# Where the weight combinations of a Strassen-like product are made, which engine starts the v loads, and the order of the five products

## The chip, the cores and the metric

The kernel runs on one core of a Trainium2 chip. The metric is device time in microseconds of one launch. The kernel before took 1371.44 us, the median of 3 runs (1368.53 to 1373.01).

## What is computed

Three layers follow one another, all in float32. B = 8, H = 8, S = 576, D = 64; 4608 tokens of width 512.

```
attention in chunks of 64 positions, per head:
  scores = q_c @ k_c^T / 8;  attn = softmax(scores);  a = attn @ v_c
x  = a as [4608, 512]
h  = x @ moe_w_in            # 512 -> 2048
g  = max(h, 0) + log1p(exp(-|h|))        # softplus
x2 = g @ moe_w_out           # 2048 -> 512
h2 = max(x2 @ w1, x2 @ w2, x2 @ w3)      # 512 -> 768, three times
out = h2 @ moe2_w_out        # 768 -> 512
```

The weights of the layers come in as 64-bit floats.

## The kernel before

A float32 number is kept as two float32r parts, hi and lo; a product is three matmul passes, hi x hi, hi x lo and lo x hi. The tokens are cut into 9 blocks of 512. TensorE's work is written in this order:

1. Blocks 0 to 2 run the first feed-forward layer plainly (mlp1), beside attention and beside the conversion of the weights from 64 bits.
2. Blocks 3 to 8 are three pairs, q = 0, 1, 2 (strassen, line 1690). The first matrix product of a pair (x @ w_in) is done in 8 units of 7 half-size products each (UnitA), with combined weights that lie in DRAM (wac, wae) and are loaded for each pair by GpSimd's queue into a ring. Between the units stand, for pairs 0 and 1, the output products of the pair's first block (mlp1_out), and after the units those of the second block; for that second block the activations go to DRAM and come back (gd). In some units a group of attention products is put in (attention(..., apart=True)).
3. For pair 2 the second matrix product (g @ w_out) is done by seven products too (class Sevens, line 1246): two of them (along) beside the units, the other five (step) after them, each in four parts n2 = 0 to 3. They are named 5, 6, 3, 4 and 7 and run in that order. Each needs activation differences, made on VectorE from raw tiles (split), and weights of its own: for 5, 6, 7 and 3 these are sums and differences of quarters of w_out, made by combos (line 1192) and stored to DRAM as wso; for 4 they are a plain quarter of w_out, which combos stores to DRAM as well. step loads them on SyncE (line 1314) into a ring of 6.
4. The gated layer takes three blocks at a time (class Triple) in 15 products, with weights combined by weights3 on VectorE and ScalarE: once for the first third of the columns (after the mark FIRST, the fifth unit of pair 1), once for the rest (after product 5 begins). They are stored as w2c; GpSimd's queue loads them again (line 1541). After the 15 products come the output products (line 1656), and the result is written.

SBUF holds 46 equal slots of 512 KB, with smaller pools beside them; a tile gets a slot of an allowed kind ("w" 32, "x" 8, "z" 4, "qh" and "vh" one each) and gives it back after its last use.

The order on each engine is not the order of the source. Each step is entered in a plan (class Plan, line 58) with a cost per engine, a latency, transfers with their time on a queue, and a due time. order() then runs a simulated clock: whenever an engine is free, the ready step with the earliest due time starts. A step without a due time gets one from those that need it. `after=` orders steps on this clock alone; at run time only the data are waited for. TensorE's steps are chained in one line. Queues run in the order given to them: what stands behind a waiting transfer on SyncE or GpSimd waits too.

For the groups of attention products, q and k are loaded in a transposing pattern of 128-byte runs on SyncE, v in 256-byte runs on GpSimd (line 468, from the call in line 687); there is one v buffer, which comes free when the product of the tile before is done. The softmax result goes through DRAM and back on SyncE (pd).

The four groups of weight combinations are put in after the output products 1, 4, 7 and 10 of pair 0:

```
    COMBOS = (1, 4, 7, 10)
    MORE = (3, 0), (5, 0), (5, 0)
    FIRST = ("unit", 1, 4)
...
                if q == 0 and j in COMBOS:
                    combos(COMBOS.index(j), [o], clock[0] + 15.0)
```

Of the kernel before, what the change touches and what calls it, by code (L numbers as in the profile page):

```python
# [20 lines left out]
P = 128  # L21
# [162 lines left out]
def tile_kernel(ctx: ExitStack, tc: tile.TileContext, q, k, v, w_in, w_out, w1, w2, w3, wo2, out):  # L184
# [110 lines left out]
    NP = 3  # L295
# [238 lines left out]

    def softmax(sc, pbuf, by_head=False):
        mx, sm = Buf("mx"), Buf("mx")
# [3 lines left out]
        if sc is None:  # L540
            s3 = lambda e: XZ.t[e][:, :TB // 2].rearrange("p (c k) -> p c k", k=CH)
            for h in range(2):
                op(
                    {"D": 0.42},
                    lambda e, h=h: nc.vector.reduce_max(m4()[:, h], s3(h), axis=AX.X),
                    r=[(XZ, "XZ"[h])],
                    w=[(mx, h)],
                    alloc=[] if h else [mx, sm],
                )
            for h in range(2):  # L550
                tt_op(
                    lambda h=h: p4()[:, h],
                    lambda h=h: s3(h),
                    lambda h=h: m4()[:, h, :, None].to_broadcast([P, HP, CH]),
                    ALU.subtract,
                    [(XZ, "XZ"[h]), (mx, h)],
                    [(pbuf, h)],
                    n=0.6,
                    alloc=[] if h else [pbuf],
                )  # L560
        else:
            s4 = lambda: sc.t[:, :, :TB // 2].rearrange("p e (c k) -> p e c k", k=CH)
            op({"D": 0.69}, lambda e: nc.vector.reduce_max(m4(), s4(), axis=AX.X), r=[(sc, "s")], w=[mx], alloc=[mx, sm])
            if by_head:
                op({"D": 0.1}, lambda e: nc.vector.tensor_scalar(mx.t, mx.t, -SCALE, -DROP, ALU.mult, ALU.add), w=[mx])

                def heads(e):
                    for u in range(H):
                        nc.scalar.activation(
                            p3()[:, u], s4()[:, u // HP, u % HP], AF.Softplus, bias=mx.t[:, u:u + 1], scale=SCALE  # L570
                        )

                op({"A": 1.9}, heads, r=[(sc, "s"), mx], w=[pbuf], alloc=[pbuf])
            else:
                tt_op(
                    p4, s4, lambda: m4()[:, :, :, None].to_broadcast([P, 2, HP, CH]), ALU.subtract, [(sc, "s"), mx], [pbuf], alloc=[pbuf]
                )
        if not by_head:
            op({"A": 0.62}, lambda e: nc.scalar.activation(pbuf.t, pbuf.t, AF.Softplus, bias=drop[:, :1], scale=SCALE), w=[pbuf])
        op({"D": 0.69}, lambda e: nc.vector.reduce_sum(sm.t, p3(), axis=AX.X), r=[pbuf], w=[sm])  # L580
        op({"D": 0.1}, lambda e: nc.vector.tensor_scalar(sm.t, sm.t, 1e-9 * float(np.exp(-DROP)), None, ALU.add), w=[sm])
# [94 lines left out]
    def attention(t, after=(), apart=False):  # L676

        if t < NTILE:
# [192 lines left out]
    def weights3(late, after):  # L871
# [31 lines left out]
        def put(s, r):  # L903
# [72 lines left out]
    SEVENS = (2,)  # L976
    COMBOS = (1, 4, 7, 10)
    MORE = (3, 0), (5, 0), (5, 0)
# [208 lines left out]
    def raw_of(q, n, f, h):  # L1187
        if (q, n // 2, f, h) not in raws:
            raws[q, n // 2, f, h] = slot("x", "w", "z", dt=F32)
        return raws[q, n // 2, f, h]  # L1190

    def combos(n2, after, due):
# [4 lines left out]
        for f in range(2):  # L1197
            for nn in range(2):
# [11 lines left out]
                if f == nn == 0:  # L1210
                    in_line("pairo", o)
                if f:
                    store["s", 4, n2, nn] = op(
                        {"G": 1.0},
                        lambda e, w=w, nn=nn: nc.gpsimd.dma_start(out=wso[4][n2][:, :, nn, :], in_=w.t[:, :, HT:].bitcast(F32)),
                        r=[w],
                        after=after,
                        lat=2.0,
                        move=1.1,
                    )  # L1220
        two_of = lambda f, h: (lambda: R[f].t[:, :, h * HT:(h + 1) * HT])
        tv = lambda: t.t.rearrange("p (n c) -> p n c", n=2)

        def put(p, src, r):
            z = slot("w", "x", "z")
            hi, lo = (lambda l=l: z.t[:, l].rearrange("p (n c) -> p n c", n=2) for l in range(2))
            copy_op(hi, src, r, [(z, "h")], alloc=[z])
            tt_op(lo, src, lambda: hi().bitcast(F32), ALU.subtract, r + [(z, "h")], [(z, "l")], hold=[token], due=due)
            store["s", p, n2] = op(
# [16 lines left out]
    class Sevens:  # L1246
# [36 lines left out]
        def send(u, name, b, h):  # L1283
# [3 lines left out]
            )  # L1287

        def split(u, p, n2):
            R = {(f, h): raws[u.q, n2, f, h] for f in range(2) for h in range(2)}  # L1290
            at, src = {
                5: ((0, 0), ((0, 1), (0, 0))),
                6: ((0, 0), ((1, 1), (0, 0))),
                3: ((1, 1), ()),
                4: ((1, 0), ((1, 0), (0, 0))),
                7: ((0, 1), ((1, 1), (0, 1))),
            }[p]
            z = R[at]
            if src:
                a, b = (R[k] for k in src)  # L1300
                tt_op(lambda: wide(z.t), lambda: wide(a.t), lambda: wide(b.t), ALU.subtract, [a, b], [z], n=1.77)
            GH, GL, token = *(Buf("g", "x", "w", fresh=tile_or_slot) for _ in range(2)), Buf("ts")
            o = copy_op(lambda: wide(GH.t), lambda: wide(z.t), [z], [GH], n=1.65, alloc=[token, GH, GL])
            in_line("ts", o)
# [3 lines left out]
        def step(u, p, n2):  # L1308
            GH, GL, token = u.split(p, n2)
            at = {5: 0, 6: 1, 7: 2, 3: 3, 4: 4}[p]  # L1310
            z, ring = slot("w", "x"), Buf("ringo")
            o = op(
                {"S": 0.48},
                lambda e: nc.sync.dma_start(out=z.t.bitcast(F32), in_=wso[at][n2].rearrange("p w n c -> p w (n c)")),
                w=[z],
                alloc=[ring, z],
                after=([store["s", at, n2]] if at < 4 else [store["s", 4, n2, nn] for nn in range(2)]) + [mark["sevens", u.q]],
                lat=2.0,
                move=2.2,
            )  # L1320
            in_line("ringo", o)
            bufs = {5: u.y, 3: u.y, 6: u.acc[:1], 7: u.acc[:1], 4: u.acc[1:]}[p]
# [3 lines left out]
            def fn(e):  # L1326
                for m in range(2):
                    for nn in range(2):
                        for wi, gi in PASS:
                            nc.tensor.matmul(  # L1330
                                dst(m),
                                z.t[:, wi, nn * HT + m * P:nn * HT + (m + 1) * P],
                                (GH, GL)[gi].t[:, nn],
# [4 lines left out]

            o = mark["step", p, n2] = pe2(2.72, fn, r=[z, GH, GL], w=bufs, alloc=[b for b in bufs if b.first is None], hold=[ring, token])
            if n2 == NJ // 4 - 1:  # L1340
# [3 lines left out]
        def read(u, p, bufs):  # L1344
# [10 lines left out]
            if p == 5:  # L1355
                keep(22)
            elif p == 6:
                keep(12)
# [120 lines left out]
    class Triple:  # L1479
# [47 lines left out]
        def product(u, s, d, alloc=()):  # L1527
# [162 lines left out]
    def strassen():  # L1690
# [19 lines left out]
        for q in range(pairs):  # L1710
# [123 lines left out]
    for n, (b, j, first, last) in enumerate(steps):  # L1834
        if n >= NJ and n % (NJ // HP) == 0:
            t = HP + n // (NJ // HP)
            t = 2 * HP + (n - NJ) // 2
            while tiles <= t + 1 and tiles < 22:
                attention(tiles, [first_loads[tiles if tiles < 2 * HP + 3 else NJ - 1]])
                tiles += 1  # L1840
        h = mlp1(b, j, first, last)
        if b == NP - 1 and j % 2 == 0:
            weightsa(j // 2, [before_last], lead)
# [41 lines left out]
```

## Time and profile before

| | |
|---|---|
| median of 3 runs | 1371.44 us (1368.53 to 1373.01) |
| the profiled execution, its own time | 1368.65 us |
| its span in the trace | 1366.8 us |
| TensorE busy | 1331.3 us, 97% |
| VectorE, ScalarE, GpSimd busy | 1002.6, 505.8, 323.9 us |
| moved by DMA | 293.56 MB, 215 GB/s over the span |

The profile is one execution. A span begins with the first instruction and ends with the last; the execution's own time is 1.85 us more. Line numbers are those of the kernel; most copies and sums are made by two helpers, lines 281, 283 (copies) and 288 (sums, differences), so that a row is told by its tiles: s is a slot, g and tmp small tiles, acc, ph, one and both accumulators. "issue" is time in which an engine waited for nothing that the profile shows.

### The profile page before, as it was taken

Reading aid. Unit: us, or ns where it says so; the run is one execution under the profiler, and the core shown is the slowest. Engines: PE = TensorE matmul, PEld = TensorE weight load, DVE = VectorE, ACT = ScalarE, POOL = GpSimd, SP = SyncE. Lnnn points to the kernel's source line nnn. Section 1 sums busy time; section 2 is a strip of 40 time slices with the busy share of each in tenths; the row PEclk is TensorE's granted clock in tenths of the full one; section 3 lists DMA queues with packets and bytes.
Section 4 is the critical chain, followed back from the end, with each engine's and each line's share of the span. In section 5 each row is a group of like instructions: output and inputs, shape, how many; then the busy total and the mean of one; then the engine's idle time right before and its main releaser. Section 6 shows DMA issues by size and latency. Waiting matters only on the chain.

```text
span 1366.8 us, 22719 instructions
## 1 busy us (share of the span) xinstructions
PE 1331.3 (97%) x8616; PEld 1091.1 (80%) x8616; DVE 1002.6 (73%) x1551; ACT 505.8 (37%) x793; POOL 323.9 (24%) x568
## 2 busy tenths in 40 slices
PE   5899999999999999999999999999999999999998
PEld 3788888888888778777788887888888888888886
DVE  8999976797676998658958897879714597145951
ACT  4544333354433544335535553432123222132211
POOL 2011545542233324323231122121101122011100
PEclk9899999999999999999999999999999999999999
DMA  8655567676788999887886799655644465344301
GB/s 273 172 165 156 126 194 202 192 261 212 202 246 258 286 327 294 266 282 257 337 296 223 249 345 364 232 192 208 212 149 162 139 231 202 143 147 154 139 30 63
DMA packets 220253, 293.56 MB, mean 215 GB/s; under 512 B 121984, under 2 KB 147008, under 8 KB 220144
## 3 DMA queue, kind: packets, MB, share of 16 engines
q0 software_dynamic: 54400, 180.31, 38.3%
q1 hardware_dynamic: 164928, 111.02, 27.0%
q8 instruction: 68, 1.11, 0.3%
q10 hardware_dynamic: 816, 0.79, 0.2%
q14 instruction: 41, 0.34, 0.1%
HBM read 198.71 MB, written 93.32 MB: 214 GB/s over the span
## 4 chain that ended last, share of the span: by engine, by line
PE 86%; DMA 6%; DVE 5%; SPq 2%; issue 1%; ACT 0%; POOL 0%; DVEq 0%; ACTq 0%; POOLq 0%
PE acc L1558 14%; PE both L1558 13%; PE acc L816 9%; PE acc L1410 9%; PE ph L796 9%; PE ph L1109 8%; PE one L1109 6%; PE both L1656 6%; PE acc L1656 5%; PE acc L1330 2%; PE acc L1263 2%; DVE s L288 2%; DMA rk<-in_k_dram 1%; PE ph L1330 1%; PE aps L503 1%
## 5 line engine op out<-in xcount | busy, mean ns | idle before, releaser
L288 DVE TENSOR_TENSOR s<-s,s 128x1024 fp32r<-128x1024 f32 (+3 forms) x216 | 208.7, 990 | 24.9 <-ACT s L281 11.7
L1410 PE MATMUL acc<-g,s 128*128 128x512 f32 x768 | 184.8, 393 | 3.7 <-DVE g L288 3.7
L1410 PEld LDWEIGHTS acc<-g,s 128*128 128x128 f32 x768 | 142.6, 188 | 35.8 <-DVE g L288 5.8
L1109 PE MATMUL ph<-s,s 128*128 128x512 f32 x576 | 144.3, 390 | 3.0 <-DMA s<-wac 2.1
L796 PE MATMUL ph<-s,s 128*128 128x512 f32 x576 | 141.2, 396 | 0.0
L816 PE MATMUL acc<-g,s 128*128 128x512 f32 x576 | 139.6, 391 | 0.0
L1109 PEld LDWEIGHTS ph<-s,s 128*128 128x128 f32 x576 | 107.9, 188 | 26.2 <-DMA s<-wac 2.6
L796 PEld LDWEIGHTS ph<-s,s 128*128 128x128 f32 x576 | 108.8, 190 | 23.4
L816 PEld LDWEIGHTS acc<-g,s 128*128 128x128 f32 x576 | 107.4, 188 | 22.7
L1541 POOL DMA_DIRECT2D s<-w2c x105 | 55.9, 532 | 278.1 <-PE both L1558 87.5
L281 ACT CAST g<-s 128x1024 fp32r<-128x1024 f32 (+1 forms) x68 | 62.2, 914 | 159.8 <-PE both L1558 36.3
L1558 PE MATMUL acc<-s,s 128*128 128x512 f32 x452 | 120.3, 389 | 0.0
L281 ACT CAST s<-s 128x512 fp32r<-128x512 f32 (+1 forms) x100 | 82.1, 832 | 91.5 <-DVE s L288 32.2
L1558 PE MATMUL acc<-g,s 128*128 128x512 f32 x400 | 110.0, 389 | 0.0
L1109 PE MATMUL one<-s,s 128*128 128x512 f32 x432 | 106.6, 390 | 1.2 <-DVE tmp L288 0.7
L1558 PE MATMUL both<-s,s 128*128 128x512 f32 x400 | 106.3, 389 | 0.0
L1558 PE MATMUL both<-g,s 128*128 128x512 f32 x368 | 100.1, 389 | 0.0
L1558 PEld LDWEIGHTS acc<-s,s 128*128 128x128 f32 x452 | 84.9, 188 | 17.6
L1109 PEld LDWEIGHTS one<-s,s 128*128 128x128 f32 x432 | 80.9, 188 | 19.1 <-DVE tmp L288 1.5
L288 DVE TENSOR_TENSOR g<-tmp,g 128x512 fp32r<-128x512 f32 x104 | 71.1, 684 | 33.2 <-ACT g L281 33.1
L468 POOL DMA_DIRECT2D rv<-in_v_dram x102 | 62.1, 613 | 115.4 <-issue 53.6
L1558 PEld LDWEIGHTS both<-s,s 128*128 128x128 f32 x400 | 75.1, 188 | 15.6
(157 smaller groups left out, 2103.9 us busy)
## 6 DMA issues: line engine op xcount, KB each, us to landing
s<-w2c POOLq DMA_DIRECT2D x105, 512.0 KB, 4.4
s<-wac POOLq DMA_DIRECT2D x66, 512.0 KB, 6.5
w2c<-s POOLq DMA_DIRECT2D x45, 512.0 KB, 4.3
wac<-s POOLq DMA_DIRECT2D x24, 512.0 KB, 5.6
s<-wso SPq DMA_DIRECT2D x20, 512.0 KB, 7.2
s<-in_moe_w_dram POOLq DMA_DIRECT2D x18, 512.0 KB, 4.9
s<-x2d POOLq DMA_DIRECT2D x18, 512.0 KB, 5.6
s<-in_moe_w_in_dram SPq DMA_DIRECT2D x16, 512.0 KB, 5.1
```

What stands on the lines that cost most here:

```text
L281: nc.scalar.copy(dst(), src())
L288: return op({"D": 0.69 * n}, lambda e: nc.vector.tensor_tensor(dst(), a(), b(), f), r=r, w=w, **kw)
L468: dma(out=dst().rearrange("p (c e d) -> p c e d", e=2, d=D)[half * CH:(half + 1) * CH, lo:lo + mine, h, :], in_=v[b, t % HP * 2 + h].rearr ...
L796: nc.tensor.matmul(ph.t, w[:, wi, kk * P:(kk + 1) * P], x[kk].t[:, xi], start=(kk == 0 and wi == 0 and xi == 0), stop=(kk == KD - 1 and wi ...
L816: nc.tensor.matmul(acc[m // 2].t[:, m % 2], w[:, wi, m * P:(m + 1) * P], g.t[:, gi, :], start=(first and wi == 0 and gi == 0), stop=(last ...
L1109: nc.tensor.matmul(dst(), ws.t[:, wi, col + kk * P:col + (kk + 1) * P], x[kk].t[:, xi], start=(first and kk == 0 and wi == 0 and xi == 0), ...
L1263: nc.tensor.matmul(u.acc[f].t[:, m], w.t[:, wi, m * P:(m + 1) * P], g.t[:, gi, :], start=(first and wi == 0 and gi == 0), stop=(last and w ...
L1330: nc.tensor.matmul(dst(m), z.t[:, wi, nn * HT + m * P:nn * HT + (m + 1) * P], (GH, GL)[gi].t[:, nn], start=(fresh and nn == 0 and wi == 0 ...
L1410: nc.tensor.matmul(acc[half].t[:, m % 2], w.t[:, wi, m * P:(m + 1) * P], g.t[:, gi, :], start=(first and wi == 0 and gi == 0), stop=(last ...
L1541: lambda e, k=k, z=z: nc.gpsimd.dma_start(out=z.t.bitcast(F32), in_=w2c[s][late + k]),
L1558: nc.tensor.matmul(bank.view()[:, f], ws(wi, slice(f * HT + kk * P, f * HT + (kk + 1) * P)), (XH, XL)[xi].t[:, kk], start=(first and kk == ...
L1656: nc.tensor.matmul(banks[t // 2].view()[:, t % 2], (GH, GL)[gi].t[:, f, t * P:(t + 1) * P], wo2_of[j].t[:, wi], start=(j == 0 and wi == 0 ...
```

## The change

v loads of the attention groups beside the units go to SyncE ("S") in place of GpSimd ("G"). The four groups of combinations start at other places: two after the output products 1 and 7 of pair 0, two with units 0 and 3 of pair 1, with later due times. The plain quarter for product 4 is no longer stored and loaded; the weights are read where they lie in SBUF, and stay there until then. The five products run in the order 5, 4, 3, 6, 7. Product 4 needs the difference that product 6 made before it, so it makes it itself, by one more operation for each of its four parts; 6 is added to a kept tile after 3 in place of 3 after 6. High parts of the activation splits are not made before the mark "late" of the pair. The raw activation tiles may lie in the slots "qh" and "vh" too. The first third of the gated layer's weights gets a due time. The weight loads of the first three blocks' products 2 and up are ordered behind product 7 in place of product 3. The change to softmax leaves its operations as they are for every call that the kernel makes.

```diff
-    wso = [[dram.tile([P, 2, 2, TB // 2], F32, name=f"wso{p}_{n}") for n in range(NJ // 4)] for p in range(5)]
+    wso = [[dram.tile([P, 2, 2, TB // 2], F32, name=f"wso{p}_{n}") for n in range(NJ // 4)] for p in range(4)]
...
-            loads(load_v(t, lambda: Rv.t, 0), Rv, "v", 1.6, [Rv] + vv, "G" if apart else "SG", after, lat=9.0)
+            loads(load_v(t, lambda: Rv.t, 0), Rv, "v", 1.6, [Rv] + vv, "S" if apart else "SG", after, lat=9.0)
...
-            tt_op(lo, view(r), lambda: hi().bitcast(F32), ALU.subtract, keys(r) + [(zs[0], "h")], [(zs[-1], "l")], n=n1, hold=[token])
+            tt_op(lo, view(r), lambda: hi().bitcast(F32), ALU.subtract, keys(r) + [(zs[0], "h")], [(zs[-1], "l")], n=n1, hold=[token], due=None if late else T0 + STEP * NJ * (NP + 4))
...
-    COMBOS = (1, 4, 7, 10)
+    COMBOS = (('out', 0, 1), ('out', 0, 7), ('unit', 1, 0), ('unit', 1, 3))
+    LATER = (7, 0)
+    SLACK = 0.0
...
-            raws[q, n // 2, f, h] = slot("x", "w", "z", dt=F32)
+            raws[q, n // 2, f, h] = slot("x", "w", "z", "qh", "vh", dt=F32)
...
-                if f:
-                    store["s", 4, n2, nn] = op(
-                        {"G": 1.0},
-                        lambda e, w=w, nn=nn: nc.gpsimd.dma_start(out=wso[4][n2][:, :, nn, :], in_=w.t[:, :, HT:].bitcast(F32)),
...
         def split(u, p, n2):
-            R = {(f, h): raws[u.q, n2, f, h] for f in range(2) for h in range(2)}
...
+            z = raws[u.q, n2, *{5: (0, 0), 4: (1, 0), 6: (0, 0), 3: (1, 1), 7: (0, 1)}[p]]
+            if p == 5:
+                u.change((0, 0), (0, 1), ALU.subtract, (0, 0), n2)
+            elif p == 4:
+                u.change((1, 0), (1, 0), ALU.subtract, (1, 1), n2)
+                u.change((1, 0), (1, 0), ALU.add, (0, 0), n2)
+            elif p == 6:
+                u.change((0, 0), (1, 1), ALU.subtract, (0, 0), n2)
+            elif p == 7:
+                u.change((0, 1), (1, 1), ALU.subtract, (0, 1), n2)
...
+                lambda: wide(GH.t), lambda: wide(z.t), [z], [GH], n=1.65, alloc=[token, GH, GL], after=[mark["late", u.q]]
...
+            if p == 4:
+                ws, ring = [wbuf["a", 4 * n2 + 2 * nn + 1, 1] for nn in range(2)], []
+                lhs = lambda wi, nn, m: ws[nn].t[:, wi, HT + m * P:HT + (m + 1) * P]
...
             elif p == 3:
-                c = u.keep[12]
-                for m in range(2):
-                    tt_op(lambda m=m: c.t[:, m], lambda m=m: bufs[m].t, lambda m=m: c.t[:, m], ALU.add, [bufs[m], c], [(c, m)], due=due)
-                u.send(12, u.b, 0)
+                keep(12)
+            elif p == 6:
+                u.total(12, lambda: wide(bufs[0].t), bufs, u.b, 0)
...
-                        after=[store["c", s, late + k], mark["step", *MORE[0]]],
+                        after=[store["c", s, late + k], mark["step", *(MORE[0] if s < 2 or u.q else LATER)]],
...
+                if ("unit", q, n) in COMBOS:
+                    combos(COMBOS.index(("unit", q, n)), [begin], clock[0] + 30.0)
...
-                outs.extend((sevens.step, p, n2) for p in (5, 6, 3, 4, 7) for n2 in range(NJ // 4))
+                outs.extend((sevens.step, p, n2) for p in (5, 4, 3, 6, 7) for n2 in range(NJ // 4))
...
-                if q == 0 and j in COMBOS:
-                    combos(COMBOS.index(j), [o], clock[0] + 15.0)
+                if ("out", q, j) in COMBOS:
+                    combos(COMBOS.index(("out", q, j)), [o], clock[0] + 60)
```

## Rows read from the trace of the kernel before

**Rows 1.** Busy time of each engine, share of the span, instructions.

```profile
PE 1331.3 (97%) x8616; PEld 1091.1 (80%) x8616; DVE 1002.6 (73%) x1551; ACT 505.8 (37%) x793; POOL 323.9 (24%) x568
```

**Rows 2.** Stretches: from:to, length, busy us per engine, PEclk, DMA share, GB/s.

```profile
455.00:505.00 50.00, 46.72 (x261) 37.29 (x260) 47.35 (x86) 24.83 (x44) 17.18 (x28) 1.00 0.90 312
505.00:605.00 100.00, 96.67 (x713) 78.03 (x713) 75.23 (x146) 41.87 (x77) 34.05 (x57) 1.00 0.93 285
605.00:690.00 85.00, 83.69 (x483) 68.03 (x482) 64.81 (x113) 41.25 (x75) 22.64 (x39) 1.00 0.80 279
...
815.00:840.00 25.00, 23.27 (x101) 18.30 (x100) 21.25 (x21) 10.14 (x10) 5.34 (x10) 1.00 1.02 417
840.00:1360.00 520.00, 520.00 (x2296) 430.73 (x2295) 315.52 (x283) 133.31 (x139) 71.86 (x135) 1.00 0.47 164
```

**Rows 3.** Timeline, PE and POOL: start, us, what, idle before and its releaser.

```profile
499.94 2.79 PE L1410 MATMUL acc<-g,s 128*128 128x512 f32 x11 [2.23 <-DVE g L288]
...
542.36 0.62 POOL L468 DMA_DIRECT2D rv<-in_v_dram  x1 [4.60 <-issue]
...
546.76 1.72 POOL L1034 DMA_DIRECT2D s<-wac  x3
...
555.05 1.67 PE L1109 MATMUL ph<-s,s 128*128 128x512 f32 x6 [2.13 <-DMA s<-wac]
```

**Rows 4.** Chain of waits, 455 to 520 us: start, us, what.

```profile
482.50 7.96 DMA tmp<-gd
...
497.47 1.80 DVE s L288 x3
```

**Rows 5.** Groups of VectorE instructions, 460 to 530 us: busy, mean ns, idle before.

```profile
L288 DVE TENSOR_TENSOR s<-s 128x512 f32<-128x512 f32 x20 | 13.1, 688 | 0.2 <-DMA wso<-s 0.2
```

**Rows 6.** Stretches, columns as in rows 2.

```profile
460.00:530.00 70.00, 66.72 (x408) 53.68 (x407) 65.68 (x120) 34.72 (x62) 25.14 (x42) 1.00 0.94 304
530.00:600.00 70.00, 66.67 (x523) 53.36 (x522) 47.03 (x93) 26.12 (x48) 24.35 (x40) 1.00 0.91 278
...
790.00:815.00 25.00, 25.00 (x112) 20.71 (x111) 22.82 (x21) 14.75 (x16) 6.74 (x13) 1.00 1.00 358
```

**Rows 7.** DMA issues, 460 to 530 us: count, size, median us to landing.

```profile
wso<-s POOLq DMA_DIRECT2D x16, 512.0 KB, 6.3
...
wso<-s POOLq DMA_DIRECT2D x8, 256.0 KB, 6.9
```

**Rows 8.** Groups by line, 334 to 650 us: the v loads on POOL.

```profile
L468 POOL DMA_DIRECT2D rv<-in_v_dram x76 | 46.3, 613 | 101.9 <-issue 49.8 <-PE one L588 47.1 <-PE acc L1410 3.2
```

**Rows 9.** DMA issues, 770 to 840 us, columns as in rows 7.

```profile
s<-wso SPq DMA_DIRECT2D x20, 512.0 KB, 7.2
...
s<-w2d POOLq DMA_DIRECT2D x6, 512.0 KB, 12.2
```

**Rows 10.** Groups by line, 790 to 840 us: the wide f32 sums on VectorE.

```profile
L288 DVE TENSOR_TENSOR s<-s,s 128x1024 f32<-128x1024 f32 (+1 forms) x22 | 26.3, 1222 | 3.5 <-DMA s<-w2d 2.7 <-ACT s L1139 0.7
```

**Rows 11.** Line 468 over the whole span, durations in ns: min/median/max.

```profile
L468 SPq DMA_DIRECT2D rv<-in_v_dram x18: 542/607/1550, 78.1 to 289.3; - x18
```

**Rows 12.** SyncE's queue on the timeline, 528 to 600 us.

```profile
528.13 1.68 SPq L860 DMA_DIRECT2D w2d<-tmp  x1
...
532.29 4.90 SPq L443 DMA_DIRECT2D rq<-in_q_dram  x4
...
548.11 6.12 SPq L443 DMA_DIRECT2D rq<-in_q_dram  x4
...
565.77 0.95 SPq L1151 DMA_DIRECT2D gd<-tmp  x2
575.61 1.73 SPq L751 DMA_DIRECT2D s<-pd  x4
```

**Rows 13.** Chain of waits, 540 to 605 us.

```profile
580.58 3.46 SPq L443
...
584.73 6.94 DMA rk<-in_k_dram
```

More of the change, by code (lines that the diff above doesn't have):

```diff
@@ L533, in to_x, with softmax @@
         )
-    def softmax(sc, pbuf, by_head=False):
+    def softmax(sc, pbuf, by_head=False, sums=False):
         mx, sm = Buf("mx"), Buf("mx")
@@ L549, in softmax, with heads @@
                 )
+            r = [(XZ, "X"), (XZ, "Z")]
+            one = lambda u: s3(u // HP)[:, u % HP]
+        else:
+            s4 = lambda: sc.t[:, :, :TB // 2].rearrange("p e (c k) -> p e c k", k=CH)
+            op({"D": 0.69}, lambda e: nc.vector.reduce_max(m4(), s4(), axis=AX.X), r=[(sc, "s")], w=[mx], alloc=[mx, sm])
+            r = [(sc, "s")]
+            one = lambda u: s4()[:, u // HP, u % HP]
+        if by_head:
+            op({"D": 0.1}, lambda e: nc.vector.tensor_scalar(mx.t, mx.t, -SCALE, -DROP, ALU.mult, ALU.add), w=[mx])
+            def heads(e):
+                for u in range(H):
+                    nc.scalar.activation(
+                        p3()[:, u],
+                        one(u),
+                        AF.Softplus,
+                        bias=mx.t[:, u:u + 1],
+                        scale=SCALE,
+                        accum_out=sm.t[:, u:u + 1] if sums else None,
+                    )
+            op({"A": 2.6 if sums else 1.9}, heads, r=[*r, mx], w=[pbuf, sm] if sums else [pbuf], alloc=[pbuf])
+        elif sc is None:
             for h in range(2):
@@ L561, in softmax @@
         else:
[L562 to L577, printed above, removed]
+            tt_op(p4, s4, lambda: m4()[:, :, :, None].to_broadcast([P, 2, HP, CH]), ALU.subtract, [(sc, "s"), mx], [pbuf], alloc=[pbuf])
         if not by_head:
             op({"A": 0.62}, lambda e: nc.scalar.activation(pbuf.t, pbuf.t, AF.Softplus, bias=drop[:, :1], scale=SCALE), w=[pbuf])
-        op({"D": 0.69}, lambda e: nc.vector.reduce_sum(sm.t, p3(), axis=AX.X), r=[pbuf], w=[sm])
+        if not sums:
+            op({"D": 0.69}, lambda e: nc.vector.reduce_sum(sm.t, p3(), axis=AX.X), r=[pbuf], w=[sm])
         op({"D": 0.1}, lambda e: nc.vector.tensor_scalar(sm.t, sm.t, 1e-9 * float(np.exp(-DROP)), None, ALU.add), w=[sm])
@@ L1211, in combos @@
                     in_line("pairo", o)
-                if f:
-                    store["s", 4, n2, nn] = op(
-                        {"G": 1.0},
-                        lambda e, w=w, nn=nn: nc.gpsimd.dma_start(out=wso[4][n2][:, :, nn, :], in_=w.t[:, :, HT:].bitcast(F32)),
[L1216 to L1220, printed above, removed]
         two_of = lambda f, h: (lambda: R[f].t[:, :, h * HT:(h + 1) * HT])
@@ L1227, in put @@
             copy_op(hi, src, r, [(z, "h")], alloc=[z])
-            tt_op(lo, src, lambda: hi().bitcast(F32), ALU.subtract, r + [(z, "h")], [(z, "l")], hold=[token], due=due)
+            tt_op(lo, src, lambda: hi().bitcast(F32), ALU.subtract, r + [(z, "h")], [(z, "l")], hold=[token], due=due, lat=SLACK)
             store["s", p, n2] = op(
@@ L1287, in send, with change @@
             )
+        def change(u, z, a, f, b, n2):
+            z, a, b = (raws[u.q, n2, *k] for k in (z, a, b))
+            tt_op(lambda: wide(z.t), lambda: wide(a.t), lambda: wide(b.t), f, [a, b], [z], n=1.77)
         def split(u, p, n2):
-            R = {(f, h): raws[u.q, n2, f, h] for f in range(2) for h in range(2)}
[L1291 to L1301, printed above, removed]
+            z = raws[u.q, n2, *{5: (0, 0), 4: (1, 0), 6: (0, 0), 3: (1, 1), 7: (0, 1)}[p]]
[8 more added lines that the diff above has]
+                u.change((0, 1), (1, 1), ALU.subtract, (0, 1), n2)
             GH, GL, token = *(Buf("g", "x", "w", fresh=tile_or_slot) for _ in range(2)), Buf("ts")
-            o = copy_op(lambda: wide(GH.t), lambda: wide(z.t), [z], [GH], n=1.65, alloc=[token, GH, GL])
+            o = copy_op(
+                lambda: wide(GH.t), lambda: wide(z.t), [z], [GH], n=1.65, alloc=[token, GH, GL], after=[mark["late", u.q]]
+            )
             in_line("ts", o)
@@ L1309, in step @@
             GH, GL, token = u.split(p, n2)
[L1310 to L1321, printed above, removed]
+            if p == 4:
+                ws, ring = [wbuf["a", 4 * n2 + 2 * nn + 1, 1] for nn in range(2)], []
+                lhs = lambda wi, nn, m: ws[nn].t[:, wi, HT + m * P:HT + (m + 1) * P]
+            else:
+                at = {5: 0, 6: 1, 7: 2, 3: 3}[p]
+                z, ring = slot("w", "x"), [Buf("ringo")]
+                ws = [z]
+                o = op(
+                    {"S": 0.48},
+                    lambda e: nc.sync.dma_start(out=z.t.bitcast(F32), in_=wso[at][n2].rearrange("p w n c -> p w (n c)")),
+                    w=[z],
+                    alloc=[*ring, z],
+                    after=[store["s", at, n2], mark["sevens", u.q]],
+                    lat=2.0,
+                    move=2.2,
+                )
+                in_line("ringo", o)
+                lhs = lambda wi, nn, m: z.t[:, wi, nn * HT + m * P:nn * HT + (m + 1) * P]
             bufs = {5: u.y, 3: u.y, 6: u.acc[:1], 7: u.acc[:1], 4: u.acc[1:]}[p]
@@ L1331, in fn @@
                                 dst(m),
-                                z.t[:, wi, nn * HT + m * P:nn * HT + (m + 1) * P],
+                                lhs(wi, nn, m),
                                 (GH, GL)[gi].t[:, nn],
@@ L1337, in fn @@
                             )
-            o = mark["step", p, n2] = pe2(2.72, fn, r=[z, GH, GL], w=bufs, alloc=[b for b in bufs if b.first is None], hold=[ring, token])
+            o = mark["step", p, n2] = pe2(2.72, fn, r=[*ws, GH, GL], w=bufs, alloc=[b for b in bufs if b.first is None], hold=[*ring, token])
             if n2 == NJ // 4 - 1:
@@ L1356, in read @@
                 keep(22)
-            elif p == 6:
-                keep(12)
             elif p == 4:
@@ L1841, in tile_kernel @@
         h = mlp1(b, j, first, last)
+        if ("step", b, j) in COMBOS:
+            combos(COMBOS.index(("step", b, j)), [h], T0 + STEP * (n + 4))
         if b == NP - 1 and j % 2 == 0:
```

## The prediction

> **What bounds the kernel now.** I read the engines' busy line first. TensorE is busy for 1331.3 of 1366.8 us, and no other engine is above 80% [rows 1]. The change adds and drops no matmul, so all it can touch is the 35.5 us in which TensorE stands still. I then cut the span into stretches to see where these lie [rows 2]: 3.28 us in 455 to 505, 3.33 us in 505 to 605, 1.31 us in 605 to 690, 1.73 us in 815 to 840, nothing from there to 1360. The rest, 25.9 us, lies ahead of 455 us or after 1360 us, where the change has no late operand to take away that I found. So there are 9.65 us to win, and each of these stretches has its own late operand.
>
> At 499.94 TensorE waits 2.23 us for the split of a reloaded activation [rows 3]. The chain of waits [rows 4] shows why: the load of that tile was issued at 482.50 and took 7.96 us, and right before the split VectorE ran three sums for the weight combinations (1.80 us), which nothing waited for. All four groups of combinations sit here. One group is 12 VectorE operations (4 sums of hi and lo, 4 sums and differences of quarters, 4 low parts), four are 48; at 688 ns each [rows 5] that is 33 us, or 8.3 us a group. Of the 70 us from 460 to 530 VectorE is busy 65.7 [rows 6]. In the same stretch the combinations' stores are 16 of 512 KB and 8 of 256 KB [rows 7], 10.5 MB of the 21.3 MB (304 GB/s for 70 us [rows 6]).
>
> At 555.05 TensorE waits 2.13 us for a unit's weights. On the timeline [rows 3] POOL stands idle for 4.60 us on "issue" ahead of a v load at 542.36, goes on with v loads, and only at 546.76 issues the unit's first three weight loads; 555.05 - 546.76 = 8.3 us later TensorE goes on. That is the rule in this stage: 76 v loads between 334 and 650 us keep POOL busy for 46.3 us, and of the idle time ahead of them 49.8 us is "issue" and 47.1 us a wait for the product that frees their buffer [rows 8].
>
> In 815 to 840 the 16 DMA engines are full (1.02, 417 GB/s) [rows 2]. Combined output weights take 7.2 us to land, the gate weights' parts 12.2 us [rows 9], and VectorE stands 2.7 us for those parts ahead of its f32 sums [rows 10], with splits queued behind.
>
> **The change, part by part.**
>
> *v loads to SyncE.* 76 issues leave POOL. Between 334 and 650 us it wins their 46.3 us and most of the 49.8 us; on the path that is the 2.13 us stall. SP gets the same 76. An SP issue of a v load took 607 ns at the median [rows 11]; the four q loads at 548.11 took 6.12 us, 1.53 us each [rows 12]. So a tile of the second pair, with four v loads, costs SP 2.4 to 6.1 us. SP is not idle there: from the first to the last of 17 merged rows, 528.13 to 566.72, its issues sum to 37.0 of 38.6 us; then it is free for 8.9 us, to 575.61 [rows 12]. A v load also waits in SP's queue for the product that frees its buffer, as it did on POOL, and the q, k, P and activation transfers stand behind it. Four tiles at the low end add 9.7 us against 10.5 us of free time: nothing. At the high end it is 24.4 against 10.5, 14 us late. Below nothing it can go to -1.2 us, the rest of the 3.33 us of that stretch, if k comes sooner. The row nearest to the operation itself is the SP v load's 607 ns, so I take +1.0 us, for a k load that already ends on the chain (issue held 3.46 us at 580.58, landing 6.94 us after 584.73 [rows 13]).
>
> *Two groups behind pair one, two in pair two.* 16.5 us of VectorE work and 4.2 MB of stores leave the first crowd, and the due time moves from 15 to 60 us, so a split goes ahead of the sums. I count the 2.23 us as gone (bounds 0 and the 3.3 us of the stretch). In 530 to 600 VectorE has 23 us free [rows 6], which covers 16.5 us; if that cover is gone, the price is the second rival.
>
> *Plain weights from SBUF.* Eight 256 KB stores leave 461 to 495 us, four 512 KB loads (2.1 MB, 5 us at 417 GB/s) leave 770 to 831. Eight weight tiles stay in SBUF up to the second product, two more tiles may hold activations; the 12.2 us loads of parts may begin later, but their first use is after 840. It costs four more sums on VectorE: 4 x 1.22 us = 4.9 us [rows 10] ahead of 10.9 us of matmuls. In 790 to 815 VectorE has 2.2 us left [rows 6], so between 0 (done earlier) and 2.7 us falls on the path; first operands are ready well ahead, I take 0.6.
>
> *Order 5, 4, 3, 6, 7 and the later loads.* Products 6 and 7 now follow each other on one accumulator; between them stands one product of the next stage (2.72 us), which covers the 1.22 us read. If VectorE is late there, it costs up to 1.2 us, held in the range. Weight loads for steps 2 and up wait for product 7, taking about 2 MB more out of 815 to 840. With both reliefs I count 1.2 of the 1.73 us there as gone (bounds 0 and 1.73).
>
> *Due time for early weight parts.* They are wanted from 702 us on the plan's clock instead of near 900, which may free VectorE in 605 to 690 us. I take half of the 1.31 us there, 0.65 (bounds 0 and 1.31; a loss is not excluded, up to as much).
>
> Sum: -2.13 - 2.23 - 1.2 - 0.65 = -6.2; +1.0 + 0.6 = +1.6; together -4.6 us. The profiled execution took 1368.65 us (1.85 outside its span), 2.79 under the median of three; a profile after should read about 1364.1, and the median 1371.44 - 4.6 = 1366.8 us. If all 9.65 us go it is 1361.8.
>
> **Rivals.**
>
> *SP becomes the bound (slower).* Place: SP's queue, 516 to 600 us. If v issues are stretched as the q loads were (1.38 us each: 4.90 and 6.12 us over 8 [rows 12]), four tiles add 22 us against 10.5 us free, 11.5 us late. The transposes of k, then the products, slip by that. Since activation loads also stand behind v loads at 470 to 482, the 2.23 us stays. Net: 11.5 + 0.6 - 4.0 = +8.1, 1379.5 us. It turns slower than 0.3% from 1.1 us an issue on. For it: 37.0 of 38.6 us, and the k chain. Against: SP's v loads at 607 ns each.
>
> *The crowd only moves (no change).* Two groups in 530 to 600 raise VectorE from 47.0 to 63.5 of 70 us, near the 65.7 of the stretch that stalls now; 4.2 MB go where the DMA share is 0.91 already, and their stores stand in POOL's queue ahead of unit weights, as v loads did. Pair two then stalls by about another 3.3 us, as pair one does: -4.6 + 3.3 = -1.3, 1370.1 us.
> The Trainium skill speaks for this one ("DMA: Bandwidth & Descriptors", section "Issuing engines are not separate DMA queues"): transfers started on different engines end on the same 16 DMA engines, and spreading them saves only the sequencer's time. By that rule the unit weights land no sooner for the move, the 2.13 us stay, and the sum is -2.5, 1368.9 us. The trace bears it out in the 0.93 DMA share of 505 to 605, but not in the 4.60 us for which POOL did not issue [rows 2, 3].
>
> *It doesn't do what it says.* The queues could keep the combinations together, since starts are ordered on a plan's clock; the output weights' relief alone is left, -1.2 + 0.6, 1370.8 us. This counts with the second rival.
>
> **How the numbers follow.** Forecast 0.45 (own range 1361.8 to 1368.5), second rival and the third 0.33, SP bound 0.22. About 0.3%, 4.1 us, is what a measurement here can tell from no change. The forecast lies just under that line at 1367.3: I give faster 0.46, same 0.32, slower 0.22. The range reaches from all stalls gone, less a little scatter, to the first rival: 1361 to 1379.
>
> **What would show it.** Right: no v load on POOL after 334, no wait of 2 us near 500 and 555, less than 0.6 us in the output products, TensorE idle for about 5 us between 455 and 1360 us. Wrong: waits of transposes for k or q in pair two, SP rows without gaps past 600 (first rival); POOL waiting for sums ahead of unit weights, VectorE at 90% in 530 to 600 with new stalls (second); a wait of product 7 for the accumulator's read.

## The result and the profile after

The changed kernel takes 1381.86 us (median of 6 runs, 1379.55 to 1388.84) against 1369.27 us for the kernel before beside it: ratio 1.0104, 95% interval 1.0078 to 1.0129. It is slower by about 1%, where 1366.8 us was predicted. One run of e11 below, 1915.55 us at a granted clock of 0.66, was in a slow state and is left out of its ratio.

The profiled execution took 1387.49 us, 5.6 us above the median, so what its rows add up to is more than the median's loss of 12.6 us. Its busy line, answering to [rows 1]:

```profile
PE 1338.5 (97%) x8616; PEld 1098.2 (79%) x8616; DVE 1007.6 (73%) x1561; ACT 500.5 (36%) x787; POOL 271.6 (20%) x484
```

The span is 1385.7 us, 18.9 longer. With the same 8616 matmuls TensorE is busy 7.2 us longer and idle for 47.2 in place of 35.5 us: 11.7 us of waiting and 7.2 us of slower work. The stretches after, columns as in [rows 2], with one that the prediction never asked for:

```profile
330.00:455.00 125.00, 118.83 (x858) 96.77 (x857) 70.43 (x139) 46.75 (x84) 15.18 (x27) 0.97 0.76 223
455.00:505.00 50.00, 45.05 (x305) 36.66 (x303) 43.37 (x83) 23.64 (x44) 3.72 (x7) 0.93 0.80 233
505.00:605.00 100.00, 94.55 (x699) 77.14 (x698) 76.78 (x145) 41.53 (x77) 20.25 (x35) 0.98 0.95 294
605.00:690.00 85.00, 81.79 (x469) 66.55 (x468) 61.60 (x114) 35.85 (x64) 13.09 (x23) 0.98 0.81 273
815.00:840.00 25.00, 25.00 (x112) 20.67 (x112) 25.00 (x26) 12.86 (x14) 4.69 (x10) 1.00 0.92 353
```

The kernel before had no idle TensorE in 330 to 455 us, the first pair:

```profile
330.00:455.00 125.00, 125.00 (x960) 102.51 (x959) 81.10 (x159) 51.24 (x93) 38.18 (x64) 1.00 0.85 250
```

After, 6.17 us are lost there, and 1.67, 2.12 and 1.90 us more than before in the next three stretches. The 1.73 us of 815 to 840 are gone. The longest waits of TensorE between 66 and 1360 us (total, times, longest):

```profile
PE acc L1419 <- ACT tmp L281: 7.7, 2, 4.7
PE one L597 <- DMA s<-pd: 4.8, 2, 2.7
PE acc L1419 <- ACT g L281: 3.5, 1, 3.5
PE one L597 <- DMA gd<-tmp: 3.3, 1, 3.3
```

The stalls on its timeline, columns as in [rows 3]:

```profile
389.58 1.02 PE L597 MATMUL one<-s,rv 64*64 64x64 f32 x27 [2.66 <-DMA s<-pd]
...
447.57 4.79 PE L1419 MATMUL acc<-g,s 128*128 128x512 f32 x12 [3.50 <-ACT g L281]
...
483.01 32.80 PE L1419 MATMUL acc<-g,s 128*128 128x512 f32 x132 [4.73 <-ACT tmp L281]
...
564.39 0.63 PE L597 MATMUL one<-s,rv 64*64 64x64 f32 x27 [2.16 <-DMA s<-pd]
...
600.50 0.99 PE L597 MATMUL one<-s,rv 64*64 64x64 f32 x29 [3.28 <-DMA gd<-tmp]
...
670.06 5.22 PE L1419 MATMUL acc<-g,s 128*128 128x512 f32 x16 [3.00 <-ACT tmp L281]
```

Neither stall of [rows 3] is there, neither the split at 500 nor the unit's weights at 555. New ones stand in their place: softmax results (s<-pd, SyncE) and ScalarE's copies. The row at 600.50 names a store, since the profile puts a wait down to what came last; that product reads s and rv only, and the loads of s were issued just ahead of that store (590.67 to 594.23), so the softmax result is the likelier cause. ScalarE was itself held. Its waits between 330 and 505 us hold a row that names another SyncE transfer, the store of an activation tile:

```profile
ACT tmp L281 <- DMA gd<-tmp: 12.1, 3, 7.7
```

A tmp tile comes free when its store to gd has landed; until then ScalarE cannot empty TensorE's accumulator. The copies that did so, ahead of the stalls at 447.57 and 483.01:

```profile
446.41 0.58 ACT L281 COPY tmp<-ph 128x512 f32<-128x512 f32 x1 [7.71 <-DMA gd<-tmp]
...
482.38 0.58 ACT L281 COPY tmp<-acc 128x512 f32<-128x512 f32 x1 [1.76 <-DMA gd<-tmp]
```

All these transfers start in SyncE's queue, here ahead of the first stall (start, us, what):

```profile
365.04 0.41 SPq L755 DMA_DIRECT2D pd<-s  x1
...
369.67 7.92 SPq L443 DMA_DIRECT2D rq<-in_q_dram  x6
377.64 0.90 SPq L760 DMA_DIRECT2D s<-pd  x2
378.63 4.04 SPq L468 DMA_DIRECT2D rv<-in_v_dram  x6
382.72 1.10 SPq L760 DMA_DIRECT2D s<-pd  x2
383.86 0.94 SPq L443 DMA_DIRECT2D rq<-in_q_dram  x2
384.89 0.39 SPq L1162 DMA_DIRECT2D gd<-tmp  x1
385.48 3.65 SPq L443 DMA_DIRECT2D rk<-in_k_dram  x2
389.22 0.42 SPq L755 DMA_DIRECT2D pd<-s  x1
```

From 369.67 us on the rows leave no gap over 0.2 us. Six v loads stand between the first half of the softmax result and the second, for which the product at 389.58 waits.

The slower work is the clock's. Stretches of 5 us around two of the stalls:

```profile
385.00:390.00 5.00, 2.34 (x26) 1.68 (x28) 0.69 (x1) 2.08 (x4) 0.77 (x1) 0.96 1.08 355
390.00:395.00 5.00, 5.00 (x70) 4.25 (x63) 3.36 (x9) 0.69 (x3) 0.00 (x0) 0.70 0.77 221
...
480.00:485.00 5.00, 1.99 (x5) 1.60 (x6) 3.91 (x8) 2.24 (x6) 0.00 (x0) 0.67 0.74 207
485.00:490.00 5.00, 5.00 (x16) 3.98 (x15) 2.70 (x6) 2.38 (x4) 0.00 (x0) 0.64 0.70 146
```

Behind a stall of 2.66 us and within and behind one of 4.73 us the granted clock reads 0.64 to 0.70: between the two levels, 1.2 and 2.4 GHz, so for part of each stretch the lower one. Behind the shortest of the six stalls, 2.16 us, it stayed up:

```profile
565.00:570.00 5.00, 5.00 (x57) 4.16 (x48) 1.60 (x5) 0.65 (x2) 0.00 (x0) 1.00 1.03 263
```

The 768 matmuls of line 1419 (line 1410 before) show what that adds, 191.1 us busy after:

```profile
L1419 PE MATMUL acc<-g,s 128*128 128x512 f32 x768 | 191.1, 403 | 11.4 <-ACT tmp L281 7.7
```

and 184.8 us before:

```profile
L1410 PE MATMUL acc<-g,s 128*128 128x512 f32 x768 | 184.8, 393 | 3.7 <-DVE g L288 3.7
```

### The profile page after: what moved, and what is told of

Its sections match the earlier page's. It is cut to its first block, busy times and chain, and to the rows that moved or that the text cites. A ratio compares the mean times of both kernels' runs of the same rounds, so it can differ in the third digit from the quotient of the medians.

```text
span 1385.7 us, 22686 instructions
## 1 busy us (share of the span) xinstructions
PE 1338.5 (97%) x8616; PEld 1098.2 (79%) x8616; DVE 1007.6 (73%) x1561; ACT 500.5 (36%) x787; POOL 271.6 (20%) x484
## 4 chain that ended last, share of the span: by engine, by line
PE 59%; DMA 2%; issue 2%; DVE 2%; SPq 1%; ACT 0%; POOL 0%; DVEq 0%; ACTq 0%; POOLq 0%
PE acc L1567 14%; PE both L1567 13%; PE acc L1419 7%; PE both L1665 6%; PE ph L1120 5%; PE acc L1665 5%; PE one L1120 4%; PE acc L1342 2%; PE acc L1265 2%; PE ph L1342 2%; DMA gd<-tmp 1%; DVE s L288 1%; PE one L597 1%; DMA w2c<-s 0%; SPq L760 0%
## 5 line engine op out<-in xcount | busy, mean ns | idle before, releaser
L288 DVE TENSOR_TENSOR s<-s,s 128x512 fp32r<-128x512 f32 (+3 forms) x222 | 214.2, 992 | 17.6 <-ACT s L281 6.0
L1419 PE MATMUL acc<-g,s 128*128 128x512 f32 x768 | 191.1, 403 | 11.4 <-ACT tmp L281 7.7
L1419 PEld LDWEIGHTS acc<-g,s 128*128 128x128 f32 x768 | 148.0, 195 | 44.8 <-ACT tmp L281 8.0
L825 PE MATMUL acc<-g,s 128*128 128x512 f32 x576 | 139.6, 391 | 0.0
L825 PEld LDWEIGHTS acc<-g,s 128*128 128x128 f32 x576 | 107.4, 188 | 22.8
L281 ACT CAST g<-s 128x1024 fp32r<-128x1024 f32 (+1 forms) x64 | 58.7, 919 | 160.7 <-PE acc L1567 45.4
L1567 PE MATMUL acc<-g,s 128*128 128x512 f32 x400 | 110.0, 389 | 0.0
L1567 PEld LDWEIGHTS acc<-g,s 128*128 128x128 f32 x400 | 75.1, 188 | 15.6
```

The source lines that it names most:

```text
L281: nc.scalar.copy(dst(), src())
L288: return op({"D": 0.69 * n}, lambda e: nc.vector.tensor_tensor(dst(), a(), b(), f), r=r, w=w, **kw)
L825: nc.tensor.matmul(acc[m // 2].t[:, m % 2], w[:, wi, m * P:(m + 1) * P], g.t[:, gi, :], start=(first and wi == 0 and gi == 0), stop=(last ...
L1419: nc.tensor.matmul(acc[half].t[:, m % 2], w.t[:, wi, m * P:(m + 1) * P], g.t[:, gi, :], start=(first and wi == 0 and gi == 0), stop=(last ...
L1567: nc.tensor.matmul(bank.view()[:, f], ws(wi, slice(f * HT + kk * P, f * HT + (kk + 1) * P)), (XH, XL)[xi].t[:, kk], start=(first and kk == ...
```

## The experiments

Twelve kernels, each timed beside the kernel before (1369 to 1370 us each time). The theory: SyncE's in-order queue is overfilled by the v loads. Rivals: the combinations or the last part of the change cost the time; VectorE's crowd only moved; any queue would do as badly.

| kernel | ratio to before | 95% interval |
|---|---|---|
| the change | 1.0104 | 1.0078 to 1.0129 |
| e1 change, v on GpSimd | 0.9998 | 0.9983 to 1.0013 |
| e2 before, v on SyncE | 1.0154 | 1.0133 to 1.0175 |
| e3 change, v on ScalarE's queue | 1.0173 | 1.0146 to 1.0200 |
| e4 change, v on either | 1.0086 | 1.0062 to 1.0110 |
| e5 e1 without the due time | 0.9976 | 0.9962 to 0.9989 |
| e6 change, k on GpSimd | 1.0236 | 1.0220 to 1.0251 |
| e7 change, each v load in two | 1.0245 | 1.0224 to 1.0265 |
| e8 before, combinations moved | 1.0045 | 1.0026 to 1.0064 |
| e9 before, last part alone | 0.9989 | 0.9969 to 1.0010 |
| e10 before, due time alone | 1.0044 | 1.0026 to 1.0063 |
| e11 change without the due time | 1.0121 | 1.0068 to 1.0174 |
| e12 change, v on SyncE in pair two only | 1.0002 | 0.9989 to 1.0015 |

**e1 and e2: one letter, both ways.** e1 takes the v loads back, e2 moves nothing else.

```diff
# e1 against the changed kernel; e2 makes the opposite edit in the kernel before
- ... 1.6, [Rv] + vv, "S" if apart else "SG", after, lat=9.0)
+ ... 1.6, [Rv] + vv, "G" if apart else "SG", after, lat=9.0)
```

> The changed kernel with one part undone: the v loads of the groups beside the units go through GpSimd's queue again. Theory 1 (SyncE's queue is the cause: 76 more issues in an in-order queue that was 37.0 of 38.6 us full, so that softmax results, q, k and activations come late): all 12 to 13 us of the loss go, and what the other parts of the change give or cost stays, 1364 to 1371 us against 1369 before. Theory 2 (two groups of weight combinations beside pair 2's units, or the new order of the five products, is the cause): still 1379 to 1383 us.

> The kernel before with one part of the change done alone: v loads of the groups on SyncE. Theory 1: as slow as the changed kernel or slower, since all four groups of combinations still crowd behind pair 1: 1379 to 1386 us, with waits of TensorE's attention products for softmax results and of activation splits. Theory 2: 1367 to 1371 us, the unit weights of pair 2 a little earlier.

e1 ran 1370.09 us and e2 1391.21. The loss comes with the letter and goes with it. e2 lies 5 us above its expected range. With v on GpSimd all the rest of the change nets to nothing (e1); with v on SyncE it is worth 0.5%, e2 against the change, so the parts do not simply add. In e1 ScalarE has no row of waiting for gd, and TensorE has no idle time in 330 to 455:

```profile
330.00:455.00 125.00, 125.00 (x960) 102.47 (x959) 80.90 (x158) 51.21 (x93) 38.16 (x64) 1.00 0.83 250
455.00:505.00 50.00, 48.94 (x273) 39.75 (x272) 49.54 (x90) 24.51 (x44) 11.61 (x20) 1.00 0.93 276
505.00:605.00 100.00, 99.51 (x731) 81.33 (x730) 68.94 (x133) 42.56 (x77) 33.46 (x57) 1.00 0.88 281
605.00:700.00 95.00, 88.87 (x488) 71.33 (x487) 74.56 (x135) 42.18 (x76) 26.31 (x44) 0.96 0.79 279
```

The second and third lines show the predicted gain: 3.28 and 3.33 us of idle have become 1.06 and 0.49. The fourth shows where it went: 6.13 us idle, where [rows 2] have 1.31 up to 690.

Is the queue late, or are the transfers slow? DMA issues in 330 to 505 us (count, KB, median us to landing), in the change:

```profile
s<-pd SPq DMA_DIRECT2D x32, 64.0 KB, 2.1
```

and in e1:

```profile
s<-pd SPq DMA_DIRECT2D x36, 64.0 KB, 3.9
```

At the median the softmax result lands faster after the change, once issued. It is issued later: between the starts of its store (pd<-s) and of its first load (s<-pd), for stores from 340 to 460 us, lie 5.5 to 9.8 us before and, from the first v loads on, 10.7 to 16.7 us after (12.6 us from 365.04 to 377.64, and 17.7 us to the second half, in the rows above). But the half for which TensorE stood at 389.58, issued from 382.72 on, was slow as well (the same view, 381 to 385 us):

```profile
s<-pd SPq DMA_DIRECT2D x2, 64.0 KB, 6.6
```

In 385 to 390 us the DMA share was 1.08. These rows do not say how much of that stall is the transfer's; the next experiment changes the issues and leaves the bytes.

**e7: the number of issues, with the same bytes.**

```diff
# every v load of the groups, in the middle
+ cut = [(0, len(mine))] if parity or t < 22 or len(mine) < 2 else [(0, len(mine) // 2), (len(mine) // 2, len(mine))]
- for h in range(2):
+ for h, (c0, c1) in ((h, c) for h in range(2) for c in cut):
```

> The changed kernel with each of these v loads cut into two of half the size: the same bytes and runs, twice the issues (76 more at 0.6 us, 46 us of SyncE's queue). Theory 1a (issue time on SyncE makes the loss): the loss of 12.6 us grows by about as much again, 1390 to 1398 us. Theory 1b (the transfers, not their issue, fill the queue): within 3 us of the changed kernel, 1379 to 1385 us.

1402.48 us, 20.6 above the change (1.4% by the ratios) for 64 more issues (158 against 94 over the span) and not one byte more, 4 us above the expected range. Its longest waits are for the softmax result:

```profile
PE one L598 <- DMA s<-pd: 11.4, 5, 4.8
```

So SyncE's own time for issues does cost, though the plan orders its lists anew here too. The Trainium skill ("DMA: Bandwidth & Descriptors", section "Issuing engines are not separate DMA queues") says that starting DMAs on several engines saves only the sequencer's time, usually small beside the transfer. For one load the trace agrees: a v load holds SyncE for 607 ns at the median and lands 4.0 us after its issue. What no single load shows is that in a queue with little room these times add up, here to 1% of the kernel in the change and 2.5% in e7.

**e6, e3 and e4: other ways to share the issues.** e6 swaps k for v, e3 gives v to ScalarE, e4 lets the plan choose between SyncE and GpSimd.

```diff
# e6: two letters
- ... "k", 2.2, [] if more else [Rk], "S" if apart else "G", ...
+ ... "k", 2.2, [] if more else [Rk], "G", ...
# e3: "A" for v; e4: "SG" for v
```

> The changed kernel, v on SyncE, but the k loads of the same groups on GpSimd in exchange: SyncE carries as many issues as before, GpSimd as many 128-byte runs as it had 256-byte runs and more. Theory 1 (what counts is how much stands in SyncE's queue, not that it is v): most of the loss goes, 1366 to 1373 us. Theory 2 (v itself must not be on SyncE, since it waits there for the buffer that the product before it frees and holds the rest): still 1378 to 1384 us.

> The changed kernel with the v loads issued by ScalarE, whose queue carries nothing else here. Theory 1a (it is the in-order sequencer of SyncE, what stands behind a v load waits): most of the loss goes, 1365 to 1372 us, unless ScalarE, held some 46 us by 76 issues, is late itself. Theory 1b (it is the transfers, 256-byte runs sent by a hardware queue instead of GpSimd's, which take DMA time from the others): as the changed kernel, 1379 to 1384 us.

> The changed kernel with each v load on SyncE or GpSimd, as the plan finds one free. Theory 1: the fewer v loads on SyncE, the smaller the loss, so between the changed kernel and the one with v on GpSimd: 1366 to 1376 us. Theory 2: 1379 to 1383 us, as the changed kernel.

All three missed. e6 took 1401.25 us. Its first pair is nearly whole again (0.37 us idle in 330 to 455), as theory has it, but pair two lost 20.5 us: now GpSimd is late. Its k loads, 330 to 650 us:

```profile
L443 POOL DMA_DIRECT2D rk<-in_k_dram x80 | 48.7, 611 | 112.7 <-issue 79.5 <-DVE s L699 16.4 <-DVE g L288 6.7
```

[rows 8] show such "issue" time for v too (49.8 us for 76 loads); here it is longer, 79.5 us for 80. Unit weights stood behind it (one wait of TensorE of 8.6 us for s<-wac), and a store of combined weights, wso, for which ScalarE waited 10.66 us ahead of the other long stall, 9.0 us. e3 took 1392.1 us: no idle in 330 to 455, so the same transfers from another queue do not stall pair one. But the issues held ScalarE's own work, five of them for 7.67 us from 451.52, and its copies came late (waits of TensorE for its g, tmp and s: 6.8, 5.1, 4.4 us). e4, with 37 of the 76 loads on SyncE, took 1381.39 us with no idle in 330 to 455 and 0.56 us in 455 to 505; 7.23 us of its time is one stall at 881 us behind a copy of ScalarE, which had stood 9.60 us on "issue". The cause of that is open, so e4 tells nothing certain of SyncE.

**e12: which pair.** The prediction looked for room on SyncE in pair two alone. In e12 the first seven groups (42 loads) stay on GpSimd, the last seven (34) go to SyncE.

```diff
- ... "S" if apart else "SG", after, lat=9.0)
+ ... ("S" if t >= 29 else "G") if apart else "SG", after, lat=9.0)
```

> The changed kernel with v on GpSimd for the first seven groups of attention products (pair 1 of the strassen stage, up to 505 us) and on SyncE for the last seven (34 of the 76 loads), which is the only place that the prediction's SyncE term looked at. Theory A (only the place was missed: SyncE's queue is full in pair one, 101 of 125 us in 330 to 455 before the change, and has room in pair two): 1369 to 1373, within 3 us of e1_after_v_gpsimd, with no idle TensorE in 330 to 455 us and under 2 us in 505 to 605. Theory B (the size was off too: also 34 loads in pair two make SyncE late): 1374 to 1379, with 3 to 6 us of idle in 505 to 605 us and waits for s<-pd or for k and q there.

1369.57 us, ratio 1.0002 where e1 has 0.9998: 34 loads cost 0.5 us by these ratios, with a scatter of some 2. So the other 42 make up 1.0104 - 1.0002, 14 us, by difference; no run has them alone on SyncE. They may also worsen what follows: in the change three of the six stalls lie in pair two (564, 600 and 670 us), and e12 has none that names a SyncE transfer.

```profile
330.00:455.00 125.00, 125.00 (x961) 102.53 (x960) 80.80 (x157) 52.05 (x95) 37.62 (x64) 1.00 0.83 244
...
505.00:605.00 100.00, 96.20 (x708) 78.22 (x707) 69.46 (x135) 42.06 (x77) 18.91 (x33) 0.98 0.92 277
605.00:700.00 95.00, 91.31 (x514) 73.62 (x512) 72.53 (x131) 43.08 (x79) 19.21 (x33) 1.00 0.80 273
```

The last two lines have 3.80 and 3.69 us idle, against 0.49 and 6.13 in e1: 7.5 and 6.6 together. The 3 to 6 us that the second theory expected in the one stretch are there, as one wait on "issue" at 544.87, but the next stretch gives most of them back and the total stays with the first theory.

**e5, e8 to e11: the rest, one edit at a time.**

```diff
# e10 is the kernel before with this line; e5 is e1 and e11 the change without it
- ... [(zs[-1], "l")], n=n1, hold=[token])
+ ... [(zs[-1], "l")], n=n1, hold=[token], due=None if late else T0 + STEP * NJ * (NP + 4))
# e8: the kernel before with the new COMBOS and their calls alone
# e9: the kernel before with the edits of Sevens, raw_of and product (LATER) alone
```

> The kernel of e1 (changed kernel, v on GpSimd) with one more part undone: the first third of the gated layer's weights gets no due time. In e1 TensorE stood 6.1 us in 605 to 690, where it stood 1.3 before, and in 505 to 605 only 0.5 in place of 3.3. Theory 1 (the early due time puts those weights' sums ahead of activation splits on VectorE, and that eats what the moved combinations gave): the stalls of 605 to 690 fall to 1 to 2 us, 1363 to 1366 us. Theory 2 (VectorE and the DMA are simply full there, with two groups moved towards it): 1368 to 1372 us as e1.

> The kernel before with only the due time on the first third of the gated layer's weights. Theory A (the due time itself costs, as e1_after_v_gpsimd against e5_vG_no_due suggests): 1372 to 1376, with idle in 605 to 700 us up from 1.3 to 4 us or more and waits there for splits on VectorE. Theory B (it cost 5 us only beside the moved combinations): 1368 to 1371, idle there under 2.5 us.

> The changed kernel with only the due time undone; v stays on SyncE. If the costs add up (SyncE about 12 to 17 us, due time about 5): 1374 to 1379, and 3 to 8 us under the changed kernel. Rival (in the changed kernel SyncE's late transfers hide what the due time costs): 1380 to 1384, as the changed kernel.

> The kernel before with one part of the change alone: two groups of combinations behind pair 1, two beside units 0 and 3 of pair 2, with the later due times; the plain quarter is still stored and loaded, v stays on GpSimd. If the crowd of 455 to 530 us is what costs the 6.6 us of 455 to 605: 1362 to 1366 us. If the crowd only moves: 1367 to 1371 us.

> The kernel before with only the second product's edits of pair 2: plain weights from SBUF, order 5, 4, 3, 6, 7, the later weight loads, the raw tiles' slots; v on GpSimd, combinations and due time as before. Theory A (each edit is worth what it changes locally: moving the combinations costs, this part gains): 1362 to 1366, idle of 815 to 870 us under 0.8 us, idle of 455 to 605 us as before (6 to 7 us). Theory B (the gain of e5_vG_no_due came from its combinations, which need the rest): no faster than the kernel before, 1368 to 1372.

The due time alone costs 0.44%, 6.0 us (e10), and 0.22%, 3.0 us, between e5 and e1, whose intervals just overlap. e10's stretch 605 to 700 has 6.52 us idle. e10 was expected to show waits for splits on VectorE; instead ScalarE waits 5.41 us for a store of the combined gated weights, w2c, which GpSimd could issue only behind v loads; its copy for TensorE stands behind. ScalarE on e10's timeline:

```profile
647.37 0.62 ACT L281 CAST s<-s 128x512 fp32r<-128x512 f32 x1 [5.41 <-DMA w2c<-s]
```

GpSimd there:

```profile
641.35 1.25 POOL L468 DMA_DIRECT2D rv<-in_v_dram  x2 [3.33 <-PE one L1109]
643.82 0.62 POOL L468 DMA_DIRECT2D rv<-in_v_dram  x1 [1.22 <-PE acc L1410]
644.42 1.12 POOL L917 DMA_DIRECT2D w2c<-s  x2
```

and TensorE:

```profile
649.01 4.44 PE L1410 MATMUL acc<-g,s 128*128 128x512 f32 x12 [4.08 <-ACT tmp L281]
```

In the change itself, taking the due time away gave nothing that can be told (e11, three runs, a wide interval, above both expected ranges). That would fit, since with v on SyncE no v load stands ahead of those stores, but it is not shown.

The combinations' move alone is slower by 0.45% (e8, a miss), though the stretch 455 to 505 went from 3.28 to 1.06 us idle: the wait for unit weights grew to 3.9 us, and 605 to 700 has 3.79 us idle. The last part alone gives 0.11%, within its interval of nothing, between its two expected ranges (e9). Both together, e5, are the only version that is faster than both kernels: 1364.74 us, 0.24% under before. Alone the two make +6.2 and -1.5 us by their ratios, together -3.3. They do not add. Every edit makes the plan order all lists anew; whether that is why, and which reordering makes the difference, is not settled.

## Why the prediction was wrong

**The step that failed** is the SyncE term: "so I take +1.0 us". The right answer was the first rival, "SP becomes the bound", which had 0.22; its 1379.5 us is near the measured 1381.86, partly by luck, since it is +8.1 from a median of 1371.44 where the loss measured is +12.6 from 1369.27. Its place and point were wrong all the same: 516 to 600 us, deciding "from 1.1 us an issue". Nothing of the kind was needed, and of its signs TensorE shows no wait for k or q. The issues took what was predicted, 607 ns at the median (the 76 loads after 334 us):

```profile
L468 SPq DMA_DIRECT2D rv<-in_v_dram x76: 486/607/1424, 357.6 to 652.8; - x76
```

What was missed is the first pair, where 42 of the 76 loads are. The term comes out near for pair two (+0.5 us in e12, with a scatter of some 2). Its "four tiles" of four loads are groups of six, six and four there, 535 to 576 us on GpSimd's timeline before; that this makes 16 too is luck. For pair one it was never worked out. There the sum was to be had from the trace of before: 51 rows of SyncE's queue in 330 to 455 us, rows like these on its timeline, sum to 101.2 of 125 us:

```profile
375.30 5.24 SPq L443 DMA_DIRECT2D rk<-in_k_dram  x8
380.64 0.38 SPq L746 DMA_DIRECT2D pd<-s  x1
381.12 0.59 SPq L860 DMA_DIRECT2D w2d<-tmp  x1
381.81 4.18 SPq L1151 DMA_DIRECT2D gd<-tmp  x2
388.38 1.73 SPq L751 DMA_DIRECT2D s<-pd  x4
390.16 4.13 SPq L443 DMA_DIRECT2D rq<-in_q_dram  x8
```

A group there comes every 19.0 us (the first v load of each starts from 355.46 to 469.75 us in six steps on GpSimd's timeline before), with eight q and eight k loads. The 19% that were free are 3.6 us a group; six v loads at 607 ns are 3.6 us, and after the change they took 3.96 to 4.86 us up to 470 us. That leaves no room in an order that also has to wait for data, and what stands behind comes late: TensorE waited 2.7 us for a softmax result, ScalarE up to 7.7 us for a store to free its tile. The queue need not be solid for that: after the change its rows in the same stretch sum to 112.3 of 125 us. Nor does the share alone decide: in e1 they sum to 45.5 of 50 us in 455 to 505, where TensorE lost 1.06 us.

**Why the range failed too.** The high end of the term, 14 us, is what pair one did cost. With it in the place of +1.0 the sum is +8.4, 1379.8 us; I kept it as a bound of pair two, gave it no chance of its own, and let the range end at the first rival, 1379. The clock was no term either: 7.2 of the 18.9 us of the profiled execution are slower work behind stalls.

**Where it was right.** The stall for unit weights is gone (no wait for s<-wac between 66 and 1360 us after); with v on GpSimd it is back, 0.5 us in e1 and 3.3 in e5. The split's at 500 is gone too: e1, e5 and e8 have 1.06 to 1.60 us idle there, a gain of 1.7 to 2.2 where 2.23 was taken. 815 to 840 is free, though 1.00 us comes back as a stop on "issue" at 858.58, and e9's -1.5 us holds the -0.6 of the last part in its interval. But "the crowd only moves" was right about the sum: in e1 the 5 us won before 605 are lost again by 700, and the ratio is 0.9998. e5, without the due time, has 7.85 us idle from 330 to 700 against 7.92 before.

**The due time had the wrong sign.** I took -0.65 us, since VectorE would be relieved; measured +3 to +6 with v on GpSimd. As far as e10 shows, the step failed because it looked at VectorE only and not at the stores that the earlier work would put into GpSimd's queue, behind the v loads.

## What to carry to other kernels

Before a load moves to another queue, add up that queue's rows over every stage in which the load occurs, and compare the free time of one period with the issues of one period. A crowded in-order queue may not show in its own transfers, which here landed faster at the median; look for how late they are issued, and for an engine that waits for a store to free its tile, and follow it to TensorE. An earlier due time moves DMA issues too: ask what they will stand behind.

## What was not expected of the hardware

TensorE's clock fell with five of the six stalls, those of 2.66 to 4.73 us (the lowest 5 us of each read 0.64 to 0.76). With the sixth, 2.16 us, it read 1.00. In all its work took 7.2 us longer, while the kernel before, whose longest stall between 330 and 1360 us was 2.23 us, kept 1.00 in every stretch of [rows 2]. In these two executions a microsecond of added waiting cost 1.6 on the mean: 18.9 us for 11.7.

On GpSimd loads in short runs come with idle time that nothing in the profile explains: 46.3 us busy and 49.8 us of "issue" for 76 v loads [rows 8], 48.7 and 79.5 us for 80 k loads in e6. On SyncE a v load is 607 ns, with gaps of at most 0.2 us around it in the rows shown.
